# The first attention's output, row tiles 3 to 21: transposed by a crossbar transfer instead of TensorE

## The chip, the cores and the metric

The kernel runs on one core of a Trainium2 chip. The core has five engines that run at the same time, each through its own list of instructions in order: TensorE (PE, the matrix array, with its weight loads as PEld), VectorE (DVE), ScalarE (ACT), GpSimd (POOL) and SyncE (SP, which here only issues transfers). Transfers between the chip's main memory and the on-chip memory, or within the on-chip memory, run on 16 DMA engines that all queues share. Matmuls write PSUM, a small memory[...], and only VectorE and ScalarE can bring results from there to the on-chip memory in this kernel. The metric is the device time of one execution in microseconds, lower is better.

## The reference

Two attentions follow one another. The first takes q, k and v of 4 batches, 8 heads, 768 positions and 64 channels, and looks at the last 96 positions and the first 8, with a bias by distance. The second takes the first one's output x (4 x 768 x 512), routes each row to two of four experts and sums their causal attentions.

```python
scores = scale * np.matmul(q, k.transpose(0, 1, 3, 2))
keep = is_global | is_local                      # first 8 keys, or 0 <= i - j < 96
scores = np.where(keep, scores + bias, -1e9)
attn = np.matmul(softmax(scores), v)             # B, H, S, 64
x = attn.transpose(0, 2, 1, 3).reshape(B, S, 512)

logits = x @ w_gate                              # two best of four experts, softmax over the two
for e in range(4):
    q, k, v = x @ wq[e], x @ wk[e], x @ wv[e]    # 512 -> 64
    ye = causal_softmax(q @ k.T / 8) @ v @ wo[e]
    out += weight_of(e) * ye
```

## The kernel before

The 4 x 768 rows are 24 row tiles of 128, numbered u = 0 to 23, six for each batch. A row tile goes through these stages; each is a small function, and its two-letter name stands in the table that orders the work.

- *Loads* (`lk`, `lq`, `lv`, line L230): 256 KB of k, q or v each, as 128 rows of 8 heads with runs of 256 bytes. The letter at the end gives the queue that issues: `s` for SP, `a` for ACT. Each of k, q and v has six buffers.
- *Casts to fp16* (`kc`, `qc` at L250; `vc` at L258, four quarters) on POOL, VectorE or ScalarE, by the letter `g`, `v` or `a`.
- *Transposes of k and q* (`tk`, `tq`, L266) on TensorE, with one copy out of PSUM (L275).
- *Local and global scores* (`sa`, `sb`, `gs`) into PSUM tiles `sps` and `gps`, exponentials on ScalarE (L345, L318).
- *Values* (`vg`, `va`, `vb`, L356 and L371) into the PSUM tile `zps`. When the last of them is through, VectorE takes the reciprocal of the sums (L378) and multiplies (L380), which gives the row tile of x in fp16, `x16`, with three buffers.
- *Transpose of x* (`tx`, L386): four 128x128 transposes on TensorE into the PSUM tile `xps`, and one copy to `xT` (L390) on VectorE or ScalarE, also three buffers. The 512 channels are split as channel = 4c + k, so each of the four transposes reads every fourth channel of a row.
- *Projections* (`pk`, `pq`, L401; `pv` with the gate, L415): the only users of `xT`. They write the PSUM tiles `pps` and `vps`, which ScalarE or VectorE copies out.
- *Routing* (`ro`), *causal scores* (`ca`, `cb`, `cc`, L446, exponentials at L449), *mask* (`ma`, L461), *values* (`za`, `zb`, L474, again into a `zps` tile), *transpose of z* (`tz`, L491), *output* (`ou`, L502 and L505) and the store of 256 KB, issued by SP.

The order of the work is written out in the string `ORDER`, some 850 entries made by a planner. The stages are called in that order, and each engine gets its instructions in it. An engine never takes a later instruction before an earlier one, so an entry that waits holds all later entries of its engine: this holds for SP, too, where a transfer that waits holds the loads behind it.

Three pools of PSUM matter: `psS` (two buffers, scores), `psZ` (one buffer, `zps` of both attentions) and `psT` (two buffers, shared by `tp`, `xps`, `pps`, `vps`, `ztps` and `ops`).

Of the kernel before, what the change touches and what calls it, by code (L numbers as in the profile page):

```python
# [9 lines left out]
F16 = mybir.dt.float16  # L10
I32 = mybir.dt.int32
Alu = mybir.AluOpType
# [6 lines left out]
P = 128  # L19
# [3 lines left out]
def kernel(  # L23
# [7 lines left out]
    nc = tc.nc  # L31
    mm = nc.tensor.matmul
    V, S_, G = nc.vector, nc.scalar, nc.gpsimd
# [5 lines left out]
    B, H, S, Dh = q.shape  # L39
# [4 lines left out]
    NK = D // P  # L44
# [8 lines left out]
    HG = H // 2  # L53
# [7 lines left out]
    ident = const.tile([P, P], F16)  # L61
# [121 lines left out]
    pp = fast.enter_context(tc.tile_pool(name="pp", bufs=3))  # L183
# [25 lines left out]
    def held(name, u):  # L209
        t, n, owner = rings[name]  # L210
        assert owner[u % n] == u
        return t[:, u % n]
# [11 lines left out]
    fs, kqT, kgs, vgs, ags, xTs, kqs, lgs, wts, a2s, as_, done = ({} for _ in range(12))  # L224
    s16s, zs_, x16s, routing, zss, zts, tps, ppss, zs2 = ({} for _ in range(9))
# [134 lines left out]
    def local_values(u, i):  # L360


        b, ri = divmod(u, NT)
        assert done[u] > i
        for hq in (2 * i, 2 * i + 1):
            for prev in range(2 if ri else 1):
                for c in range(2):
                    for hf in range(2):
                        r = slice(hf * KB, hf * KB + KB)
                        at = c * (2 * P - KB) + prev * P  # L370
                        mm(zs_[u][:, hf, hq * VW:(hq + 1) * VW],  # L371
                           lhsT=as_[u - prev][r, hq % 2, hq // 2, at:at + P],
                           rhs=held("vbuf", u - prev)[r, c, hq, :], start=False, stop=True,
                           skip_group_check=True)
        if i == 1:
            z4 = zs_[u][:, :, 0:HG * VW].rearrange("r a (h d) -> r a h d", h=HG)
            rinv = rinv1[:, b, ri, :].rearrange("r (a h) -> r a h", a=2)
            V.reciprocal(rinv, z4[:, :, :, Dh])  # L378
            x16s[u] = pp.tile([P, 2, HG, Dh], F16, name="x16")
            V.tensor_tensor(x16s[u][:, :, :, :], z4[:, :, :, 0:Dh],  # L380
                            rinv.unsqueeze(3).to_broadcast([P, 2, HG, Dh]), op=Alu.mult)

    def turn_x(u, on):
        x_ps = psT.tile([P, NK, P], F16, name="xps", tag="t")
        for j in range(NK):
            nc.tensor.transpose(x_ps[:, j, :],  # L386
                                x16s[u][:, :, :, :].rearrange("r a h d -> r (a h d)")
                                .rearrange("r (c k) -> r k c", k=NK)[:, j, :], ident[:, :])
        xTs[u] = pp.tile([P, NK, P], F16, name="xT")
        copies[on](xTs[u][:, :, :], x_ps[:, :, :])  # L390

    def project_qk(u, i, on=None):
# [149 lines left out]
    def general_path(ctx):  # L542
# [190 lines left out]
        "tk": (turn, 0), "tq": (turn, 1), "sa": (local_scores, 0), "sb": (local_scores, 1),  # L733
        "gs": (global_scores,), "vg": (global_values,),
        "va": (local_values, 0), "vb": (local_values, 1), "tx": (turn_x,),
        "pk": (project_qk, 0), "pq": (project_qk, 1), "pv": (project_v,), "ro": (route,),
        "ca": (causal_scores, 0), "cb": (causal_scores, 1), "cc": (causal_scores, 2),
# [11 lines left out]
    for i, r in enumerate((rinv1, rinv2)):  # L749
        r = r[:, :, :, :].rearrange("p b t h -> p (b t h)")  # L750
# [22 lines left out]


ORDER = """
wi4a lq0s qc0g lk0a kc0g wm17 tk0 lv0a lk1a vc0g lq1s xt0 lk2s xb0 xg0 kc1g lq2a lk3a lq3s lq4s
qc1g tq0a wm12 vs0 az0 gi0 tk1 tq1v lk4a gs0 wm3 gs1 kc2g lv1s az1 az2 lk5s wm1 sa0 lv2s qc2g
sb0 kc3v lq5a qc3v qc4g tk2 tq2v tk3 tq3v vg0 wi0s wi1s va0 vb0 az3 az4 kc4g kc5v vc1g gs2 lv3a
lv4s vc2g sa1 sb1 wc0g tk4 wc1g tq4v vg1 sa2 sb2 lk6s wi2s va1 qc5a vb1 sa3 sb3 tx0v tk5 tq5v
vg2 va2 vb2 gs3 sa4 tx1v tx2v sb4 lq6a lq7s lk7s lk8s lv5a pk0 pk1 vc3v sa5 vc4g wc2g sb5 lq8s  # L780
kc6a lq9s lk9s lk10s pq0v pq1v vg3 va3 vb3 pk2 pq2a ca0 ca1 vg4 va4 qc6v qc7g tk6 tq6v vb4 pv0a
pv1a ca2 cb2 vg5 tx3v kc7g tk7 tq7v ma0 kc8g lv6a qc8v gi1 pk3 vc5g pq3a pv2v ro0 sa6 sb6 tx4v
ro0 qc9g tk8 tq8v kc9g va5 vb5 ca3 lq10s lq11s lk11s pv3v kc10g pv4a sa7 vc6g ro0 gs4 lv7s ma1
qc10v lv8s tk9 lq12s tq9v tk10 tq10v lk12a ro0 vs1 sb7 qc11v pk4 kc11v ro0 pq4a tx5v vg6 lq13s
vc7g va6 vb6 vc8g ro0 sa8 ro0 qc12g sb8 tk11 tq11v lk13s lk14s pv5v vg7 ca4 va7 cb3 vb7 tx6v
lq14s pk5 pq5a lq15s za0 lv9s lv10s zb0 lk15s sa9 sb9 lv11s qc13g lk16s ro1 tx7v pk6 pq6a kc12g
kc13v kc14g tk12 tq12v ro1 lq16s za1 zb1 sa10 sb10 tz0v tk13 tq13v lq17s ca5 vg8 va8 gi2 lk17s
vb8 pv6a lq18s qc14g ro1 pv7v lk18a lk19s gs5 cb4 lv12s tx8v ma2 qc15g za2 zb2 vc9g tk14 tq14v
kc15g vc10g pv8a cb5 ro1 ro1 cc4 vg9 va9 ma3 vb9 kc16g pk7 pq7a qc16v kc17g tk15 tq15v ro1
lk20s ro1 ro2 sa11 sa12 vg10 va10 vc11g vb10 gs6 tx9a wi3s tk16 tq16v qc17g qc18v sb11 sb12  # L790
lv13s lv14s za3 vc12g tx10v lq19s pk8 wc3g pq8v ma4 tz1a lq20s zb3 sa13 sa14 tz2v pk9 kc18v
pq9v kc19a pv9a vs2 vg11 va11 vb11 lk21s cc5 tk17 kc20g tq17v tk18 tq18v gi3 vg12 ca6 va12 vb12
sa15 lv15s vc13g ou0a ou1v ca7 ca8 tx11v za4 tx12v zb4 ou2a pk10 pq10v sb13 sb14 vc14g pv10v
pv11v ro2 ro2 ro2 vg13 cb8 va13 vb13 gs7 lv16s lk22s tz3a ma5 ro2 sb15 ro2 qc19g pk11 pq11a
tz4a lq21s lq22s lk23s ro2 vg14 ro3 ro3 vc15g va14 vb14 ca9 qc20g ma6 cb9 qc21g tx13v ro3 tk19
tq19v ma7 ma8 za5 zb5 ou3v ou4v sa16 sa17 kc21g vg15 va15 vb15 pv12a lv17s lv18s tx14v lv19s
sb16 sb17 za6 lv20s lq23a tk20 tq20v zb6 pv13a ca10 cb10 pk12 pq12v vc16g pk13 za7 kc22g zb7
pq13a ro3 vc17g vc18g tk21 tq21v gs8 ro3 vg16 va16 cc10 vb16 tz5a tx15v qc22g sa18 ma9 sa19
tz6v qc23g za8 zb8 ou5a ou6v ca11 ca12 ro3 vg17 va17 vb17 pk14 ro3 pq14v lv21s pv14v sb18 sb19
tz7v za9 zb9 tz8a tx16v vs3 sa20 tk22 ro4 tq22v ou7a vg18 va18 vb18 cb11 cc11 vc19g ou8v pk15  # L800
pq15v kc23g ma10 za10 zb10 pv15a lv22s tk23 tq23v sb20 sa21 tx17v ma11 ma12 za11 tx18v ro4
lv23s zb11 tz9a ro4 ca13 ro4 ma13 ca14 tz10v pk16 pq16v tz11v ca15 vg19 va19 vb19 pv16v pv17v
vc20g cb14 cb15 ro4 vg20 ro4 ro4 va20 vb20 pk17 pq17a tx19v gs9 sa22 ou9v za12 zb12 tx20a sb21
sb22 ou10v ou11a vg21 vc21g va21 vc22g vb21 ro5 sa23 sb23 vc23g pv18v pk18 za13 ro5 zb13 pq18a
ro5 ro5 pv19v ca16 ca17 ro5 ro5 vg22 va22 ro5 ma14 tz12v pk19 pq19v tx21a ca18 vb22 cb16 pk20
pq20v tx22v vg23 cc16 va23 vb23 pv20a ro6 pv21a cb17 cc17 ma15 ro6 ma16 ro6 za14 tz13v zb14
pk21 ma17 pq21v ou12a za15 zb15 ou13a ma18 tx23v ca19 ca20 ro6 tz14v ro6 tz15v za16 zb16 pv22v
pv23a cb20 ca21 ro6 ro6 za17 tz16v ro7 ro7 zb17 ou14a pk22 ma19 pq22v ro7 ro7 cb21 za18 zb18
pk23 pq23a ro7 ma20 tz17v ro7 ca22 za19 zb19 ro7 cb22 ma21 ou15v ou16v ca23 za20 zb20 tz18v
cc22 ou17v cb23 za21 zb21 ou18a tz19v ma22 cc23 za22 tz20v tz21a zb22 ou19a ou20v ma23 za23  # L810
tz22v zb23 ou21a ou22a tz23v ou23a
"""

MAXB = 512
# [38 lines left out]
```

## Time and profile before

The median of three runs is 154.23 us (153.66 to 155.45). The profiled execution spans 151.9 us.

| what | value |
|---|---|
| DMA bytes | 27.81 MB, mean 183 GB/s |
| SP's queue (q1) | 65,632 packets, 23.60 MB, 60.0% of 16 engines |
| ACT's queue (q10) | 14,704 packets, 3.68 MB, 10.8% |
| loads of k, q, v issued by SP, by ACT | 58, 14 |
| issue to landing of a load, median | 5.0 to 6.0 us |
| issue to landing of an output, median | 2.1 us |
| transposes of x (L386) | 96 matmuls, busy 9.5 us |

Busy time of an engine is the sum of its instructions' records. On TensorE the records of following matmuls overlap, so a group's busy time is not what it costs the array; the distance between starts is. "Idle before" names what the engine was waiting for ahead of a group. The line of DMA shares gives, for each of 40 equal slices, how full the 16 DMA engines were in tenths.

### The profile page before, as it was taken

Reading aid. Unit: us, or ns where it says so; the run is one execution under the profiler, and the core shown is the slowest. Engines: PE = TensorE matmul, PEld = TensorE weight load, DVE = VectorE, ACT = ScalarE, POOL = GpSimd, SP = SyncE. Lnnn points to the kernel's source line nnn. Section 1 sums busy time; section 2 is a strip of 40 time slices with the busy share of each in tenths; the row PEclk is TensorE's granted clock in tenths of the full one; section 3 lists DMA queues with packets and bytes.
Section 4 is the critical chain, followed back from the end, with each engine's and each line's share of the span. In section 5 each row is a group of like instructions: output and inputs, shape, how many; then the busy total and the mean of one; then the engine's idle time right before and its main releaser. Section 6 shows DMA issues by size and latency. Waiting matters only on the chain.

```text
span 151.9 us, 7115 instructions
## 1 busy us (share of the span) xinstructions
PE 137.3 (90%) x2987; PEld 107.5 (71%) x2987; DVE 111.3 (73%) x343; ACT 105.6 (70%) x174; POOL 94.6 (62%) x258
## 2 busy tenths in 40 slices
PE   5889969989999998899999999999999999999700
PEld 4556747768789786787787887788868987856300
DVE  6976958577887984888759788797867787797610
ACT  0345656666879887498786877869796988898410
POOL 4492896484888785749889789543786444544000
PEclk9999999999999999999999999999999999999995
DMA  4999999979899898999994994345013003116540
GB/s 106 284 288 291 353 231 279 265 177 277 195 276 233 199 239 184 204 285 223 316 242 103 261 222 135 84 147 134 4 69 145 4 4 140 73 48 230 194 167 11
DMA packets 80376, 27.81 MB, mean 183 GB/s; under 512 B 75472, under 2 KB 77008, under 8 KB 80336
## 3 DMA queue, kind: packets, MB, share of 16 engines
q1 hardware_dynamic: 65632, 23.60, 60.0%
q10 hardware_dynamic: 14704, 3.68, 10.8%
q8 instruction: 25, 0.41, 1.1%
q14 instruction: 15, 0.12, 0.3%
HBM read 20.98 MB, written 6.29 MB: 180 GB/s over the span
## 4 chain that ended last, share of the span: by engine, by line
PE 61%; DMA 11%; DVE 9%; POOL 9%; issue 3%; ACT 2%; POOLq 0%; ACTq 0%; DVEq 0%
DMA qf<-in_q_dram 11%; PE pps L401 10%; PE zps L474 7%; PE ops L502 7%; PE vps L415 6%; PE cps L446 6%; PE zps L371 4%; PE sps L335 4%; POOL vbuf L258 4%; PE tp L266 4%; PE xps L386 3%; PE sps L342 3%; PE ztps L491 2%; PE zps L356 2%; POOL s16q L250 1%
## 5 line engine op out<-in xcount | busy, mean ns | idle before, releaser
L449 ACT ACTIVATE a<-cps 128x1024 f16<-128x1024 f32 (+1 forms) x48 | 42.0, 916 | 4.0 <-PE cps L446 3.6
L258 POOL CAST vbuf<-vf 64x256 f16<-64x256 f32 x92 | 37.0, 402 | 6.6 <-DMA vf<-in_v_dram 2.6
L345 ACT ACTIVATE abuf<-sps 128x636 f16<-128x636 f32 (+1 forms) x48 | 30.7, 683 | 9.1 <-PE sps L342 8.7
L461 POOL TENSOR_SCALAR_AFFINE_SELECT a<-a 128x256 f16<-128x256 f16 x48 | 18.4, 411 | 12.8 <-ACT a L449 12.8
L275 DVE COPY kqT<-tp 128x1024 f16<-128x1024 f16 x23 | 15.5, 686 | 5.3 <-PE tp L266 5.1
L380 DVE TENSOR_TENSOR x<-zps,rinv 128x512 f16<-128x512 f32 x24 | 16.6, 691 | 0.8
L474 PE MATMUL zps<-v2buf,a 128*128 128x65 f16 x336 | 15.4, 193 | 0.2
L371 PE MATMUL zps<-vbuf,abuf 64*128 64x65 f16 x704 | 15.2, 189 | 0.0
L335 PE MATMUL sps<-biasT,ident 64*64 64x318 f16 (+1 forms) x192 | 14.8, 313 | 0.1
L401 PE MATMUL pps<-xT,wk 128*128 128x128 f16 x192 | 14.6, 219 | 0.1
L401 PE MATMUL pps<-xT,wq 128*128 128x128 f16 x192 | 14.5, 219 | 0.0
L474 PEld LDWEIGHTS <-a 128*128 128x128 f16 x336 | 12.9, 97 | 2.1 <-DVE zs L485 0.8
L371 PEld LDWEIGHTS <-abuf 64*128 64x128 f16 x704 | 13.9, 94 | 0.6
L342 PE MATMUL sps<-kqT 64*64 64x159 f16 (+2 forms) x384 | 14.2, 228 | 0.0
L415 PE MATMUL vps<-wvg,xT 128*128 128x260 f16 x96 | 13.6, 275 | 0.0
L502 PE MATMUL ops<-wo,zt 128*128 128x512 f16 x48 | 13.2, 380 | 0.4 <-DVE zt L495 0.4
L250 POOL CAST s16k<-kf 128x512 f16<-128x512 f32 x17 | 10.3, 609 | 5.2 <-DMA kf<-in_k_dram 3.3
L446 PE MATMUL cps<-kq,kq 64*128 64x128 f16 x240 | 13.2, 217 | 0.0
L446 PEld LDWEIGHTS <-kq 64*128 64x128 f16 x336 | 9.9, 94 | 4.5 <-issue 3.4
L401 PEld LDWEIGHTS <-wk 128*128 128x128 f16 x192 | 11.5, 98 | 1.8 <-issue 0.2
L342 PEld LDWEIGHTS <-kqT 64*64 64x64 f16 x384 | 11.4, 108 | 1.1 <-issue 0.2
L401 PEld LDWEIGHTS <-wq 128*128 128x128 f16 x192 | 11.6, 98 | 0.1
(112 smaller groups left out, 272.9 us busy)
## 6 DMA issues: line engine op xcount, KB each, us to landing
out_dram<-osb SPq DMA_DIRECT2D x24, 256.0 KB, 2.1
qf<-in_q_dram SPq DMA_DIRECT2D x20, 256.0 KB, 5.0
vf<-in_v_dram SPq DMA_DIRECT2D x20, 256.0 KB, 5.2
kf<-in_k_dram SPq DMA_DIRECT2D x18, 256.0 KB, 5.1
kf<-in_k_dram ACTq DMA_DIRECT2D x6, 256.0 KB, 5.3
vf<-in_v_dram ACTq DMA_DIRECT2D x4, 256.0 KB, 5.8
qf<-in_q_dram ACTq DMA_DIRECT2D x4, 256.0 KB, 6.0
w<-in_moe_wk_dram SPq DMA_DIRECT2D x1, 512.0 KB, 5.1
```

The lines of the kernel that those rows point to most:

```text
L258: copies[on](o[hf * KB:(hf + 1) * KB, c, :, 0:Dh], fs["v", u][c * KB:(c + 1) * KB, hf * HG:(hf + 1) * HG, :])
L335: mm(s_ps[o, hh, 0:2 * w].rearrange("r (c n) -> r c n", c=2), lhsT=ident2[r, :], rhs=biasT[r, p, 0:w].unsqueeze(1).to_broadcast([KB, 2, w] ...
L342: mm(s_ps[o, hh, c * w:c * w + n], lhsT=kqT[b][r, 0, p, k0:k0 + KB], rhs=kqT[b][r, 1, p, k0:k0 + n], start=False, stop=True, skip_group_ch ...
L345: S_.activation(as_[u][:, :, g, :].rearrange("r h (c n) -> r h c n", c=2)[:, :, :, 0:w], s_ps[:, :, 0:2 * w].rearrange("r h (c n) -> r h c ...
L371: mm(zs_[u][:, hf, hq * VW:(hq + 1) * VW], lhsT=as_[u - prev][r, hq % 2, hq // 2, at:at + P], rhs=held("vbuf", u - prev)[r, c, hq, :], sta ...
L401: mm(p_ps[:, i, ep, :], lhsT=w[:, ko, ep, :, :].rearrange("r a d -> r (a d)"), rhs=xT[:, ko, :], start=(i == 0 and ep == 0 and ko == 0), s ...
L415: mm(v_ps[:, :], lhsT=xT[:, ko, :], rhs=wvg16[:, ko, :], start=(ko == 0), stop=(ko == NK - 1))
L446: mm(s_ps[:, e2, i, :], lhsT=kqs[b * NT + ci][r, 0, ep, :], rhs=kqs[u][r, 1, ep, :], start=(i == 0), stop=True, skip_group_check=True)
L449: S_.activation(a2[:, :, 4 * c:4 * c + len(part), :], s_ps[:, :, 0:len(part), :], func=Exp, scale=sc2)
L461: G.affine_select(out=d, in_=d, pattern=[[0, NEP], [1, P]], channel_multiplier=-1, base=0, compare_op=Alu.is_ge, fill=0.0)
L474: mm(z_ps[:, e, :], lhsT=a2[:, e % 2, (e // 2) * n + ci, :], rhs=held("v2buf", b * NT + ci)[:, e, :], start=(e == 0 and ci == 0), stop=Tru ...
L502: mm(o_ps[:, :], lhsT=zts[u][:, ep, :], rhs=wo16[:, ep, :], start=(ep == 0), stop=(ep == NEP - 1))
```

## The change

For row tiles 3 to 21 the transpose of x is a transfer from on-chip memory to on-chip memory, issued by SP, in which the crossbar of the transfer path transposes (`dma_start_transpose`). TensorE and PSUM have no part in it, and no copy follows. Row tiles 0, 1, 2, 22 and 23 stay on TensorE.

[...]the multiply L380 now writes `x16` with the channels interleaved: k first, then c. Its neighbours in the order of reading lie 128 elements apart in the result. `x16` has five buffers instead of three and `xT` four. The table is planned anew: all stages are the same, but their order, the engines of many casts and copies, and the queues of loads differ; 24 loads of k, q and v are issued by ACT and 48 by SP, and the warm-up of the exponential (`xt0`) stands at the end of the table instead of near its start.

```diff
-            x16s[u] = pp.tile([P, 2, HG, Dh], F16, name="x16")
-            V.tensor_tensor(x16s[u][:, :, :, :], z4[:, :, :, 0:Dh],
-                            rinv.unsqueeze(3).to_broadcast([P, 2, HG, Dh]), op=Alu.mult)
+            x16s[u] = pp.tile([P, NK, P], F16, name="x16", bufs=5)
+            V.tensor_tensor(x16s[u][:, :, :].rearrange("r k (a h d) -> r a h d k", a=2, h=HG),
+                            z4[:, :, :, 0:Dh].rearrange("r a h (d k) -> r a h d k", k=NK),
+                            rinv.unsqueeze(3).unsqueeze(4)
+                            .to_broadcast([P, 2, HG, Dh // NK, NK]), op=Alu.mult)
 
     def turn_x(u, on):
+
+        xTs[u] = pp.tile([P, NK, P], F16, name="xT", bufs=4)
+        if on == "s":
+            nc.sync.dma_start_transpose(xTs[u][:, :, :],
+                                        x16s[u][:, :, :].rearrange("r k c -> r (k c)"))
+            return
         x_ps = psT.tile([P, NK, P], F16, name="xps", tag="t")
         for j in range(NK):
-            nc.tensor.transpose(x_ps[:, j, :],
-                                x16s[u][:, :, :, :].rearrange("r a h d -> r (a h d)")
-                                .rearrange("r (c k) -> r k c", k=NK)[:, j, :], ident[:, :])
-        xTs[u] = pp.tile([P, NK, P], F16, name="xT")
+            nc.tensor.transpose(x_ps[:, j, :], x16s[u][:, j, :], ident[:, :])
         copies[on](xTs[u][:, :, :], x_ps[:, :, :])
```

Of the table, the entries around the transposes of row tiles 3 to 6 (the letter `s` marks the transfer):

```diff
-pv1a ca2 cb2 vg5 tx3v kc7g tk7 tq7v ma0 kc8g lv6a qc8v gi1 pk3 vc5g pq3a pv2v ro0 sa6 sb6 tx4v
-ro0 qc9g tk8 tq8v kc9g va5 vb5 ca3 lq10s lq11s lk11s pv3v kc10g pv4a sa7 vc6g ro0 gs4 lv7s ma1
-qc10v lv8s tk9 lq12s tq9v tk10 tq10v lk12a ro0 vs1 sb7 qc11v pk4 kc11v ro0 pq4a tx5v vg6 lq13s
+lq8a lk8s pq1v qc7g vg3 va3 tx2v vb3 tx3s lv5s ca0 lv6a tk6 tq6v wc2g ca1 tk7 tq7v vc4v lk9a
+vg4 lq9s pk2 pq2a sa6 gi1 sb6 qc8g pv0v pv1v va4 vb4 tx4s lq10a ca2 cb2 kc8g tk8 tq8v pk3 ma0
+ma1 lk10s pq3a vg5 sa7 lv7a sb7 vc5v vc6g pv2v kc9g lk11s ro0 ro0 pv3v gs4 va5 vb5 tx5s vs1
+qc9g tk9 lv8s ro0 ro0 pk4 tq9v pq4v vg6 va6 lq11s lq12a qc10g vb6 sa8 tx6s sb8 kc10g pv4v tk10
```

More of the change, by code (lines that the diff above doesn't have):

```diff
@@ L775 @@
 ORDER = """
[L776 to L781, printed above, removed]
@@ L782 @@
-pv1a ca2 cb2 vg5 tx3v kc7g tk7 tq7v ma0 kc8g lv6a qc8v gi1 pk3 vc5g pq3a pv2v ro0 sa6 sb6 tx4v
-ro0 qc9g tk8 tq8v kc9g va5 vb5 ca3 lq10s lq11s lk11s pv3v kc10g pv4a sa7 vc6g ro0 gs4 lv7s ma1
-qc10v lv8s tk9 lq12s tq9v tk10 tq10v lk12a ro0 vs1 sb7 qc11v pk4 kc11v ro0 pq4a tx5v vg6 lq13s
-vc7g va6 vb6 vc8g ro0 sa8 ro0 qc12g sb8 tk11 tq11v lk13s lk14s pv5v vg7 ca4 va7 cb3 vb7 tx6v
-lq14s pk5 pq5a lq15s za0 lv9s lv10s zb0 lk15s sa9 sb9 lv11s qc13g lk16s ro1 tx7v pk6 pq6a kc12g
-kc13v kc14g tk12 tq12v ro1 lq16s za1 zb1 sa10 sb10 tz0v tk13 tq13v lq17s ca5 vg8 va8 gi2 lk17s
@@ L788 @@
[L788 to L811, printed above, removed]
+lk0s lk1a kc0g wm17 tk0 az0 xb0 az1 lq0s lq1a az2 lv0a xg0 lk2s lk3a kc1a qc0g qc1g lq2s lq3a
@@ new lines @@
+wm7 tq0a qc2v tk1 wm1 tq1a wm7 sa0 vc0g az3 sb0 kc2g wm2 tk2 lk4s gi0 vs0 tq2v kc3g qc3g tk3
+kc4v lq4s qc4g lv1s vc1g lk5s kc5g gs0 gs1 lq5s lv2a vc2g tq3v sa1 sb1 wi0a wi1s lv3s vg0 va0
+vb0 tk4 sa2 wm1 vg1 lk6s lk7s az4 tq4v tx0v qc5v gs2 sb2 sa3 va1 wc0g vb1 tk5 tq5v lq6a sb3
+tx1v vc3g vg2 va2 lq7a gs3 sa4 qc6g wi2s wc1v vb2 sb4 wi4s pk0 pk1 pq0v sa5 sb5 kc6v kc7g lv4a
+lq8a lk8s pq1v qc7g vg3 va3 tx2v vb3 tx3s lv5s ca0 lv6a tk6 tq6v wc2g ca1 tk7 tq7v vc4v lk9a
+vg4 lq9s pk2 pq2a sa6 gi1 sb6 qc8g pv0v pv1v va4 vb4 tx4s lq10a ca2 cb2 kc8g tk8 tq8v pk3 ma0
@@ new lines @@
+ma1 lk10s pq3a vg5 sa7 lv7a sb7 vc5v vc6g pv2v kc9g lk11s ro0 ro0 pv3v gs4 va5 vb5 tx5s vs1
+qc9g tk9 lv8s ro0 ro0 pk4 tq9v pq4v vg6 va6 lq11s lq12a qc10g vb6 sa8 tx6s sb8 kc10g pv4v tk10
+tq10v vc7g ro0 lk12s vc8g kc11v vg7 qc11g ca3 ca4 ro0 lv9s ro0 lv10s lk13a va7 vb7 qc12g pk5
+pq5v pv5v sa9 sb9 ma2 vg8 va8 vb8 lq13s cb3 kc12g tx7s lk14s vc9g tk11 tq11v kc13g pk6 pq6v za0
+zb0 tx8s lq14a sa10 gs5 tk12 lv11s tq12v ro1 pv6a sa11 sb10 tz0v vg9 va9 qc13v vb9 ro1 cb4
+vc10g tx9s gi2 tk13 tq13v pv7v ca5 qc14v vg10 va10 vb10 lq15s lv12s cc4 pv8a kc14g tk14 ro1
@@ new lines @@
+vc11g lk15a tq14v sa12 tx10s sb11 za1 zb1 lk16a pk7 pq7v pv9a ma3 cb5 lq16s vg11 lq17s vc12g
+va11 vb11 ro1 gs6 ro1 pk8 pq8v tz1a qc15v lk17s kc15v kc16g sa13 qc16g vs2 za2 pk9 pq9a lq18s
+tx11s tk15 ro1 lv13a qc17g lv14s ro1 tq15v lk18s zb2 sb12 sb13 ro2 kc17g ro2 pk10 pq10v tk16
+tq16v wi3s ca6 vg12 va12 vb12 tx12s ro2 ca7 tk17 tq17v pv10a ro2 ma4 sa14 sb14 za3 zb3 vc13g
+tz2v lk19s lk20a pk11 ro2 kc18g sa15 lv15s ro2 lq19s lq20s sb15 pq11v wc3g pv11v vc14g cc5
+lv16a lv17s vg13 lq21s qc18g ma5 va13 vb13 ca8 ou0v ou1v cb8 ma6 kc19g lk21a za4 zb4 pk12 ro2
@@ new lines @@
+pq12a qc19v ro3 tk18 tq18v kc20v sa16 sb16 qc20g vg14 lk22s va14 tx13s vb14 sa17 tz3v tk19 ro3
+tq19v ca9 cb9 tx14s tz4v vc15g za5 zb5 ou2a tk20 tq20v gs7 sa18 za6 ro3 zb6 ou3a vc16g ou4v
+lv18s ca10 ro3 vg15 va15 vb15 kc21g kc22g cb10 pv12v pv13v cc10 qc21g lv19s vg16 va16 vb16 ca11
+tx15s tz5v pk13 pq13a ma7 lq22a za7 zb7 sb17 lv20s sb18 tz6v lq23s tk21 lv21s tq21v ma8 za8 zb8
+pv14a gi3 sa19 sa20 pk14 ro3 pq14v tz7v ma9 ro3 vg17 vc17g vc18g va17 tx16s lv22s cb11 vb17
+ou5a ou6v ro3 ro4 tx17s sb19 sb20 za9 pv15v qc22v zb9 vc19g tz8a gs8 ro4 vs3 tk22 pk15 tq22v
@@ new lines @@
+vc20g pq15a ma10 ca12 vc21g vg18 lk23s lv23s ro4 va18 vb18 cc11 pv16v pv17v ro4 tx18s ro4 za10
+qc23v zb10 ma11 ou7a sa21 ro4 ro4 sb21 pk16 pq16v tz9v vg19 ca13 ro5 kc23g va19 vb19 ca14 tk23
+ma12 ma13 tq23v pk17 pq17v cb14 vg20 va20 vb20 sa22 sb22 tx19s tx20s tz10v pv18v za11 ro5 zb11
+ro5 ou8a ou9v gs9 za12 zb12 ou10a pv19v ca15 cb15 vc22g ma14 za13 vc23g zb13 pk18 pq18v tz11v
+ca16 ro5 ro5 vg21 va21 vb21 ca17 pv20v pk19 pq19v cb16 ro5 cc16 ro5 ro6 vg22 va22 vb22 ro6 ro6
+tz12v pk20 pq20a sa23 sb23 tx21s tz13v ro6 ro6 za14 zb14 pk21 pq21a tx22v cb17 vg23 va23 ro6
@@ L812 @@
+vb23 ou11a ou12v cc17 ma15 ma16 ma17 ro6 za15 zb15 tz14a ou13v ca18 ca19 ma18 tx23v za16 zb16
+pv21a pv22v ca20 cb20 pv23v ro7 za17 tz15v zb17 ro7 tz16v ro7 ro7 ro7 ca21 cb21 pk22 ma19 ma20
+ma21 pq22v pk23 ro7 pq23a ro7 za18 zb18 ca22 ou14v ou15a za19 zb19 ca23 tz17v cb22 tz18v za20
+zb20 ou16v cc22 ou17a za21 ma22 zb21 cb23 cc23 ma23 tz19v ou18v tz20v za22 zb22 ou19a ou20v
+tz21v za23 tz22a zb23 ou21a ou22a tz23v ou23a xt0
 """
```

## Prediction

> **What bounds the kernel now.** I read the shares of the engines first, then the stretches of 20 us, then the chain that ended last, then the timeline around two of the transposes that the change takes away, then the transfer queues. The engine shares and slices say that TensorE is the fullest engine and that the transfers are full for a good half of the run:
>
> ```profile
> PE 137.3 (90%) x2987; PEld 107.5 (71%) x2987; DVE 111.3 (73%) x343; ACT 105.6 (70%) x174; POOL 94.6 (62%) x258
> ...
> PE   5889969989999998899999999999999999999700
> ...
> DMA  4999999979899898999994994345013003116540
> ```
>
> The stretches, with columns PE, weight load, DVE, ACT, POOL, granted clock, DMA share and GB/s, show the same in time:
>
> ```profile
> 0.00:20.00 20.00, 17.05 (x244) 11.88 (x245) 15.94 (x56) 8.22 (x14) 12.47 (x34) 1.00 1.10 266
> 20.00:40.00 20.00, 17.80 (x408) 14.10 (x409) 13.42 (x35) 13.47 (x24) 13.36 (x34) 1.00 1.04 240
> 40.00:60.00 20.00, 19.77 (x506) 16.78 (x504) 15.29 (x44) 16.55 (x29) 16.42 (x44) 1.00 1.00 225
> 60.00:80.00 20.00, 19.09 (x453) 15.44 (x453) 15.20 (x43) 15.40 (x29) 15.36 (x40) 1.00 1.00 250
> 80.00:100.00 20.00, 20.00 (x484) 15.88 (x482) 16.54 (x47) 15.94 (x28) 14.94 (x39) 1.00 0.61 155
> ```
>
> Up to 40 us TensorE has gaps (17.05 and 17.80 of 20) and the DMA engines have none (share 1.10 and 1.04); from 40 to 80 us both are full; from 80 us on TensorE alone is. The chain agrees: it goes through transfers of q rows three times (14.4 to 21, 24.8 to 30.3, 57.9 to 62.7 us) and from 64 to 143 us hardly leaves TensorE.
>
> ```profile
> PE 61%; DMA 11%; DVE 9%; POOL 9%; issue 3%; ACT 2%; POOLq 0%; ACTq 0%; DVEq 0%
> ```
>
> Counting each matmul by the usual distance to the next start in a dense run (56 ns for 128 columns, 111 for 260, 216 for 512, 29 and 15 ns for the two kinds of 65 columns, and so on) gives 117 us of array time in all: 63 to 76% of the first 40 us, 80 to 92% of the time from 40 to 140.
>
> So TensorE work removed after 40 us should come off the end, provided nothing else starts to hold TensorE; work removed before 40 us should not.
>
> **What a transpose costs TensorE.** Records of matmuls overlap (220 ns each in the groups), so I take the distance between starts:
>
> ```profile
> 71.08 0.41 PE L386 MATMUL xps<-ident,x 128*128 128x128 f16 x4
> 71.33 0.47 PE L474 MATMUL zps<-v2buf,a 128*128 128x65 f16 x10
> 71.63 0.39 PE L386 MATMUL xps<-ident,x 128*128 128x128 f16 x4
> 71.86 0.47 PE L474 MATMUL zps<-v2buf,a 128*128 128x65 f16 x10
> ```
>
> Four transposes hold the array for 0.25 and 0.23 us; I use 0.24 us for a row tile. The groups name the two VectorE operations around them:
>
> ```profile
> L380 DVE TENSOR_TENSOR x<-zps,rinv 128x512 f16<-128x512 f32 x24 | 16.6, 691 | 0.8
> ...
> L390 DVE COPY xT<-xps 128x512 f16<-128x512 f16 x21 | 8.7, 420 | 2.5 <-PE xps L386 2.3
> ```
>
> **What the Trainium skill says.** "DMA: Bandwidth & Descriptors", section "Latency and other measured facts", gives crossbar transposes 261 GB/s with non-contiguous middle dims and 350 to 400 when contiguous. "VectorE: DVE Perf Modes", section "The three transpose paths", gives 1309 ns for one 128x128 tile by the crossbar. No trace of the kernel before has a crossbar transpose. The first page's section "Issuing engines are not separate DMA queues" says that all issuers share the same 16 engines; the trace agrees, since the share falls from 1.22 to 0.15 only as the loads run out, whoever issued them. "Advanced Engine Details and Errata", section "SBUF Cachelines", says that accesses that touch another 16-byte line each time pay a penalty. The trace before has no VectorE write of that kind; the nearest thing, weight loads that read x with 8-byte steps, takes 113 ns against 97 to 98 for packed ones.
>
> **The change, part by part.**
>
> *Removed from TensorE:* 19 row tiles x 0.24 us = 4.6 us. The transposes before 40 us make some 5 to 6 row tiles, of which rows 0 to 2 stay as they are; so about 3 of the 19 fall where TensorE has gaps anyway. 16 x 0.24 = 3.8 us come off the part that is full.
>
> *Removed from the copies:* 16 copies of xT on VectorE (16 x 0.42 = 6.8 us) and 3 on ScalarE (3 x 0.58 = 1.7 us). The replanned table spends it again: VectorE gets 6 more copies of v2buf (2.5), 2 of kq (1.4), 3 of zt (0.9), 4 quarter casts of v (1.4), 4 of wq (about 1.6, by POOL's 0.39 each), one of q (0.5), and one kqT fewer (-0.7): +7.6, so VectorE stays where it was. ScalarE loses 6 of v2buf, 2 of kq, 3 of zt and more, some 6 us in all, and issues 25 loads instead of 15, 10 x 0.4 = 4 us. I cost all this at nothing: these engines are 70 to 73% busy and TensorE covers them. The freed PSUM pair of xps (two buffers are shared by six uses per row, now five) can only help; I leave it out.
>
> *Table call for the activation tables moved to the end:* the first ScalarE cast loads the table instead, and it stands in front of a wait for the first k load. Nothing. The 1-element activation at the end runs beside the checks of the sums on VectorE. Nothing.
>
> *The multiply (L380)* writes the same 512 elements, but each one 256 bytes from the last. At one element a cycle it stays 0.69 us. If every write costs two, the slope 1.04 ns per element (from 691 and 424 ns for 512 and 256 elements) doubles: 1.22 us. I take 0.69 and give the other end to a rival.
>
> *Added: 19 transposes of 128 KB on SP's queue.* Low end: 128 KB at 261 GB/s = 0.5 us of the engines. High end: four times 1309 ns = 5.2 us. I take about 1 us on the queue and 2 to 3 us from issue to landing with nothing ahead (the 256 KB outputs land in 2.1). 19 x 1 = 19 us on SP's queue, which now holds 60% of 152 = 91 us. The ten loads that move to ScalarE's queue take about 10 x 1.4 = 14 us off it (91 us over 65,632 packets = 1.4 us for a load of 1,024). About even, and hidden.
>
> *Added waits.* A transpose on SP's in-order queue waits for the multiply of its row and for an xT buffer (four of them, for row u-4). Behind it stand loads of k, q, v for later rows; their casts on POOL and VectorE, then turn on TensorE, wait in turn. Before, loads were issued as soon as buffers came free; now they go in step with L380. By adding the array times above along both tables, the load of a k row from row 12 to 18 stands 3 to 7 us of TensorE work before its cast now, 4 to 10 before. The medians of issue to landing are 5 us while the queue is full, so there is little to spare, but a queue that is fed less far ahead is also less full. The other wait is projection for the transposed row: from the last matmul into zps to the first projection lie 4.3 us of TensorE work at the tightest rows (4 and 5) and 5 to 10 elsewhere. The chain needs 0.2 + 0.69 + handoffs 0.3 + issue 1 + landing 2 to 3 = 4.2 to 5.2 us; at the 70 to 80% density of that stretch 4.3 of work last 5.5 to 6. It fits, with nothing left if two loads are ahead in the queue.
>
> **Forecast:** 154.2 - 3.8 = 150.4 us.
>
> **Rivals.**
>
> 1. *The waits take it back.* Ten rows, 3 to 12, fall while the queue is full; if each holds TensorE for 0.35 us, 3.5 us return: 153.9 us, no change. For it: landings of 5 us in this stretch. Against it: fewer loads ahead in the queue.
>
> 2. *The strided multiply is twice as long.* zps has one buffer, so the next values stage waits for L380. In the new table 0.7 to 2.6 us of TensorE work (median 1.4) stand between; the hold is about 1.2 us now and would be 1.7. An average stall of 0.35 us x 24 = 8 us: 154.2 - 3.8 + 8 = 158.4 us, slower. For it: the page on cachelines. Against it: at one element a cycle of 2 bytes the port is far from its peak.
>
> 3. *The crossbar is slow.* At 2.6 us for a row (half the high end) SP's queue carries 91 - 14 + 50 = 127 us, most of it beside the loads, and the path to the projection becomes about 7 us against 5 to 6: 1 to 1.5 us for each of the 10 early rows, 12 us, or 154.2 - 3.8 + 12 = 162.4. At 5.2 us the queue alone holds 176 us. For it: the 1309 ns. Against it: that price must hold a fixed part.
>
> 4. *The freed PSUM buffer and the new table give more.* By the array times above, some 27 us up to the last matmul are not work; a tenth of it (2.7) and the full 4.6: 147 us.
>
> **How the numbers follow.** Forecast 0.50, rival 4 0.06: faster 0.56. Rival 1 0.13: within 1%. Rival 2 0.14, rival 3 0.17: slower 0.31. The range goes from 147 (rival 4) to 160, beyond which lies most of rival 3 and nothing else.
>
> **What would show it.** Right: xps falls to 20 matmuls, the 3.8 us is gone between 40 us and the end, L380 stays near 0.69 us, transposes land in under 4 us, and the waits of projection for xT are few. Rival 1 shows as pps or vps waiting for the transfer of xT; rival 2 as L380 near 1.2 us and zps waiting for it; rival 3 as long landings and SP busy in them, with casts waiting for loads behind. The forecast is wrong above all if a step of the transpose that no trace here shows is mis-sized.

## Result and profile after

The changed kernel takes 180.66 us (median of 4 runs, 179.71 to 183.22) against 153.94 us before (now of 4 runs, too): a ratio of 1.174 (95% interval 1.162 to 1.186). It is 27 us slower where a gain of 4 was forecast, and 20 us beyond the upper end of the range.

The profiled execution spans 181.5 us. It is the slowest of the four by 2 us (its granted clock is 0.94 in the mean, 0.97 in the others), so the gaps counted below are a little large; ratios here and below leave such executions out, medians keep them. First the shares of the engines and the slices, the same lines as before:

```profile
PE 138.9 (77%) x2913; PEld 105.8 (58%) x2913; DVE 148.7 (82%) x346; ACT 101.1 (56%) x159; POOL 93.0 (51%) x251
...
PE   6875979677768777897785976976949866999820
...
DVE  7888598989999999888958698789897988788730
```

TensorE has 74 recorded matmuls fewer and falls from 90% to 77%. VectorE has about as many instructions as before and 37 us more work: it is now the fullest engine. The row of nines that TensorE had is gone. Two stretches from 40 us on (columns PE, weight load, DVE, ACT, POOL, granted clock, DMA share, GB/s):

```profile
40.00:60.00 20.00, 15.14 (x390) 12.53 (x389) 19.09 (x34) 10.30 (x16) 10.94 (x28) 1.00 0.89 179
60.00:80.00 20.00, 16.11 (x391) 13.24 (x392) 18.30 (x39) 12.47 (x22) 12.66 (x32) 1.00 0.90 189
```

TensorE got through 390 matmuls from 40 to 60 us, 506 before. The chain that ended last says where the time went; its shares by engine are

```profile
PE 39%; DVE 39%; DMA 11%; ACTq 3%; issue 2%; POOL 1%; ACT 1%; SPq 0%; POOLq 0%; DVEq 0%
```

VectorE's share of the chain was 9% and is 39%; its largest single item is the multiply L380 with 28%. The groups show why:

```profile
L380 DVE TENSOR_TENSOR x<-zps,rinv 128x512 f16<-128x512 f32 x24 | 58.5, 2438 | 0.8
...
L479 PE MATMUL zps<-v2buf,a 128*128 128x65 f16 x336 | 15.2, 195 | 11.0 <-DVE x L380 9.0
...
L356 PE MATMUL zps<-vg,ag 64*128 64x260 f16 x48 | 7.0, 287 | 9.8 <-DVE x L380 8.5
```

The multiply takes 2438 ns instead of 691: 24 x 1.747 = 42 us more on VectorE. The next values, of either attention, need the one `zps` buffer and wait for it. The view of TensorE's waits (total, times, longest) gives 8 + 8 such waits by name:

```profile
PE zps L479 <- DVE x L380: 9.0, 8, 1.6
PE zps L356 <- DVE x L380: 8.5, 8, 1.4
```

By the starts in the trace it is more rows still: at 20 of the 24, the next matmul into `zps` starts within 0.2 us of the end of the multiply, at 7 before. The other waits of this kind are put down to a small VectorE operation that stands behind the multiply.

A piece of the chain from 64 us, in order of time (start, length, what), shows the alternation. TensorE does the work that the table put between two users of `zps`, and the rest of its list stands behind the waiting one:

```profile
63.77 0.51 PE zps L371 x32
64.30 0.22 DVE rinv L378
64.54 2.44 DVE x L380
...
73.05 0.50 PE zps L371 x32
73.58 0.22 DVE rinv L378
73.82 2.44 DVE x L380
76.31 0.34 PE zps L479 x6
```

By starts of matmuls plus their usual distances (the prediction's way of counting), the gaps over 0.15 us in TensorE's work sum to 9.9 us in the profile before and 42.6 us after; 24.3 us of the latter lie in front of a `zps` matmul (0.5 before). The array time itself went from 116.6 to 112.6 us, so the 4 us that the change was to save were saved; they are invisible behind 33 us of new gaps.

The transfers did what was expected of them (issue on SP's queue: shortest, median, longest in ns; then the time to landing):

```profile
L389 SPq DMA_TRANSPOSE xT<-x x19: 1190/1201/2820, 35.7 to 144.8; - x19
...
DMA to landing us min/median/max: 2.4/4.0/6.7
```

### The profile page after: what moved, and what is told of

It is laid out like the page before. It is cut to its first block, busy times and chain, and to the rows that moved or that the text cites. A ratio compares the mean times of both kernels' runs of the same rounds, so it can differ in the third digit from the quotient of the medians.

```text
span 181.5 us, 6995 instructions
## 1 busy us (share of the span) xinstructions
PE 138.9 (77%) x2913; PEld 105.8 (58%) x2913; DVE 148.7 (82%) x346; ACT 101.1 (56%) x159; POOL 93.0 (51%) x251
## 2 busy tenths in 40 slices
DMA packets 90711, 30.29 MB, mean 167 GB/s; under 512 B 85808, under 2 KB 87344, under 8 KB 90672
## 4 chain that ended last, share of the span: by engine, by line
PE 39%; DVE 39%; DMA 11%; ACTq 3%; issue 2%; POOL 1%; ACT 1%; SPq 0%; POOLq 0%; DVEq 0%
DVE x L380 28%; DMA qf<-in_q_dram 8%; PE pps L406 6%; PE zps L479 6%; PE zps L371 4%; PE ops L507 4%; DMA vf<-in_v_dram 3%; PE cps L451 3%; PE vps L420 3%; ACTq L230 3%; PE sps L335 3%; DVE rinv L378 2%; DVE kqT L275 2%; PE sps L342 2%; PE ztps L496 2%
## 5 line engine op out<-in xcount | busy, mean ns | idle before, releaser
L380 DVE TENSOR_TENSOR x<-zps,rinv 128x512 f16<-128x512 f32 x24 | 58.5, 2438 | 0.8
L258 POOL CAST vbuf<-vf 64x256 f16<-64x256 f32 x88 | 35.5, 403 | 12.8 <-DMA vf<-in_v_dram 9.2
L275 DVE COPY kqT<-tp 128x1024 f16<-128x1024 f16 x22 | 16.8, 769 | 2.5 <-PE tp L266 2.4
L371 PE MATMUL zps<-vbuf,abuf 64*128 64x65 f16 x704 | 16.0, 194 | 0.0
L406 PE MATMUL pps<-xT,wk 128*128 128x128 f16 x192 | 15.4, 227 | 0.2 <-DVE kqT L275 0.2
L371 PEld LDWEIGHTS <-abuf 64*128 64x128 f16 x704 | 14.6, 97 | 1.2 <-issue 0.8
L356 PE MATMUL zps<-vg,ag 64*128 64x260 f16 x48 | 7.0, 287 | 9.8 <-DVE x L380 8.5
L250 POOL CAST s16q<-qf 128x512 f16<-128x512 f32 x16 | 9.8, 617 | 9.1 <-DMA qf<-in_q_dram 8.4
L250 POOL CAST s16k<-kf 128x512 f16<-128x512 f32 x18 | 11.1, 621 | 5.0 <-DMA kf<-in_k_dram 4.8
L411 DVE CAST kq<-pps 128x512 f16<-128x512 f32 x15 | 10.6, 709 | 3.1 <-PE pps L406 3.0
```

Of the source, the lines that this page charges most:

```text
L250: copies[on](s16s[nm, u][:, :, :], fs[nm, u][:, :, :])
L258: copies[on](o[hf * KB:(hf + 1) * KB, c, :, 0:Dh], fs["v", u][c * KB:(c + 1) * KB, hf * HG:(hf + 1) * HG, :])
L275: copies[on](kqT[b][:, :, :, ri * P:(ri + 1) * P], tps[u][:, :, :, :])
L371: mm(zs_[u][:, hf, hq * VW:(hq + 1) * VW], lhsT=as_[u - prev][r, hq % 2, hq // 2, at:at + P], rhs=held("vbuf", u - prev)[r, c, hq, :], sta ...
L380: V.tensor_tensor(x16s[u][:, :, :].rearrange("r k (a h d) -> r a h d k", a=2, h=HG), z4[:, :, :, 0:Dh].rearrange("r a h (d k) -> r a h d k ...
L406: mm(p_ps[:, i, ep, :], lhsT=w[:, ko, ep, :, :].rearrange("r a d -> r (a d)"), rhs=xT[:, ko, :], start=(i == 0 and ep == 0 and ko == 0), s ...
```

## The experiments

My theory after the result: the write order of the multiply is the whole loss; each element is written 256 bytes from the last, and that costs 3.5 times, not 1 or 2. Rivals: the short inner runs of four cost it, not the distance; the transfers; the new table.

**1. The forms of the operation by themselves.** This kernel leaves both attentions out and only runs the multiply, copies and transfers in several forms, four times each.

> Leaves out both attentions: it only times the disputed operation in several forms, four times each, and stores a tile to the output. Theory A (each write that steps to another 16-byte line costs extra): the multiply with packed writes takes 0.69 us; writes 4 and 8 bytes apart stay near 0.7; 16, 32 and 64 bytes apart rise to 2.4 us like the interleaved one; groups of four packed writes with a gap between stay near 0.7. Theory B (short innermost rows of 4 cost a start each, whatever they write): groups of four packed writes take about 2.4 us and writes far apart in long rows stay at 0.7. Reading PSUM out of order with packed writes, in two halves: 0.85 us if only writes suffer, 2 us or more if reads suffer the same. The crossbar transfer alone: 1.2 us on the queue, 2 to 3 us to land.

The groups, each shape apart. `xo<-z` with 512 elements holds four packed and four interleaved ones (4 x 691 + 4 x 2432 ns = 12.5 us), `xf` is an fp32 result, `zs` a source in on-chip memory, the 256-element form reads PSUM out of order and writes packed, L92 and L94 are ScalarE copies, interleaved and packed, L86 and L89 VectorE copies of fp16. The two lines of `big` are the groups with steps of 8 and 16 bytes, each from a window of its own:

```profile
L59 DVE TENSOR_TENSOR xo<-z,rinv 128x512 f16<-128x512 f32 x8 | 12.5, 1561 | 0.3
L92 ACT CAST xo<-z 128x512 f16<-128x512 f32 x4 | 9.7, 2432 | 75.5 <-DVE xo L89 75.4
L59 DVE TENSOR_TENSOR xo<-zs,rinv 128x512 f16<-128x512 f32 x4 | 9.7, 2423 | 0.0
L86 DVE COPY xo<-zh 128x512 f16<-128x512 f16 x4 | 5.2, 1306 | 0.1
L59 DVE TENSOR_TENSOR xf<-z,rinv 128x512 f32<-128x512 f32 x4 | 5.0, 1243 | 0.0
L59 DVE TENSOR_TENSOR xo<-z,rinv 128x256 f16<-128x256 f32 x8 | 2.9, 439 | 0.0
L94 ACT CAST xo<-z 128x512 f16<-128x512 f32 x4 | 2.3, 585 | 0.1
...
L89 DVE COPY xo<-zh 128x512 f16<-128x512 f16 x4 | 1.2, 294 | 0.1
```

```profile
L59 DVE TENSOR_TENSOR big<-z,rinv 128x512 f16<-128x512 f32 x4 | 5.2, 1290 | 0.1
...
L59 DVE TENSOR_TENSOR big<-z,rinv 128x512 f16<-128x512 f32 x4 | 9.7, 2419 | 0.1
```

| fp16 result of 512 elements, written | ns |
|---|---|
| packed; or in groups of four packed with a gap behind each | 691; 691 |
| every 2nd element (4-byte step) | 726 |
| every 4th (8) | 1290 |
| every 8th, 16th, 32nd (16, 32, 64) | 2419, 2293, 2377 |
| interleaved as in the change (256-byte step inside groups of four) | 2432 |

Groups of four cost nothing when each group is packed, so short runs are not it. The step between consecutive writes is: nearly free at 4 bytes, 1.9 times at 8, 3.3 to 3.5 times from 16 on. (At 8 bytes theory A had expected no cost.) Reading out of order costs nothing: two of the 256-element forms, with a 16-byte step in PSUM, start 0.33 us apart, while a packed 512-element form starts every 0.73 us. The source does not matter either: read from on-chip memory, the interleaved form takes 2423 ns.

The Trainium skill's page "Advanced Engine Details and Errata", section "SBUF Cachelines", names 16-byte lines and a penalty for another line at each access; the rise up to 16 bytes and its end there agree. Its remark that at least two hits on a line are needed must not be read as two being enough: at 8 bytes each line gets two, and the operation still takes 1290 ns. A price for each new line would fit the series: from 8 to 16 bytes the lines that 512 elements touch double from 256 to 512, and 1129 ns more make 4.4 ns a line, an estimate from these two figures and the page's line; packed or at 4 bytes (64 or 128 lines) that is under 0.6 us, less than the operation takes anyway. But the fp32 result and the fp16 copy touch a new line with each element, too, and take half as long (1243 and 1306 ns), so the count of lines alone does not give the time. What in the engine or the memory sets it stays open.

A transfer by itself takes 1.19 us on the queue and 2.4 us to land, and 0.6 to 0.7 us of the 16 engines.

**2. One part alone: the interleaved multiply in the kernel before,** with its own table and all transposes on TensorE (the four weight loads of a row then read packed channels).

```diff
-V.tensor_tensor(x16s[u][:, :, :, :], z4[...], ...)                  # packed
+V.tensor_tensor(x16s[u].rearrange("r k (a h d) -> r a h d k", ...), z4[...], ...)
```

> The kernel before with its table and its TensorE transposes, but with the interleaved multiply. Theory A (the multiply at 2.4 us holds the one zps buffer): each of 24 row tiles holds TensorE some 1 to 1.5 us more, 174 to 190 us. Rival (the transfers and the queue they stand in made the kernel slow): the multiply is hidden, 154 to 159 us.

182.95 us, ratio 1.188 (1.181 to 1.196): the multiply alone costs 29 us, without any transfer and without the new table. Shares and the group of this kernel:

```profile
PE 141.2 (77%) x2987; PEld 109.7 (60%) x2987; DVE 147.5 (80%) x343; ACT 106.0 (58%) x174; POOL 94.6 (52%) x258
```

```profile
L380 DVE TENSOR_TENSOR x<-zps,rinv 128x512 f16<-128x512 f32 x24 | 58.6, 2441 | 0.8
```

They are close to those of the changed kernel. Its gaps in front of `zps` sum to 26.5 us, and 5.3 us more lie in front of `xps`, which here waits for the multiply, too.

**3. The change with the multiply mended.** The channels stay interleaved, but the instruction reads PSUM out of order and writes packed, in two halves of 256:

```diff
-V.tensor_tensor(x16s[u].rearrange("r k (a h d) -> r a h d k", ...), z4 (d k) ..., ...)
+for a in range(2):
+    V.tensor_tensor(x16s[u][:, :, a*64:(a+1)*64].rearrange("r k (h d) -> r k h d", ...),
+                    z4[:, a, :, 0:Dh].rearrange("r h (d k) -> r k h d", k=NK), ...)
```

> The changed kernel with one edit: the multiply writes packed and reads PSUM out of order instead, in two halves (0.83 us for both by the forms measured). Theory A2 (what is left of the loss is in the table and in what waits behind the transfers): 158 to 163 us, as the natural-order kernel (160.6). Rival (the weights in shorter runs cost the natural-order kernel its 7 us): 149 to 154 us.

157.84 us, ratio 1.030 (1.017 to 1.043): 22.8 of the 26.7 us are gone. The multiply, now two instructions, takes 0.84 us for a row:

```profile
L381 DVE TENSOR_TENSOR x<-zps,rinv 128x256 f16<-128x256 f32 x48 | 18.1, 419 | 1.0 <-DVE rinv L378 0.2
```

The kernel is still slower than before, so the write order is not all of it. Two waits of TensorE in this kernel:

```profile
PE vps L422 <- DMA xT<-x: 3.5, 4, 1.9
PE ops L509 <- POOL wo L174: 2.8, 1, 2.8
```

No wait for the multiply is left in this view; the projections wait for transfers (landing at a median of 4.6 us here, 7.2 at most), and one output waits for `wo`, whose load stands behind a transfer on SP's queue. I also undid the interleaving altogether: channels split as 128k + c, the weights loaded to match, multiply as before.

> The changed kernel with channels in natural order: weights loaded so that channel = 128k + c, so that the multiply writes packed and the transfer still transposes contiguous blocks. Theory A: the multiply is back at 0.69 us and the time falls to 148 to 153 us, at or below the kernel before. Rival (transfers): 165 us or more, with waits for xT and for loads behind the transfers.

160.55 us, ratio 1.043 (1.035 to 1.051), where 148 to 153 us had been expected if the multiply were the whole loss. This kernel has one fault of its own: the weights then arrive in short pieces (92,336 packets under 512 B against 85,808). The same edit put into the kernel before measures that:

> The kernel before with weights loaded in natural channel order and nothing else changed. Theory A2: 153 to 155.5 us. Rival (the weights in shorter runs are the cost): 157 us or more.

155.72 us, ratio 1.016 (1.008 to 1.024). So some 2 us of the 160.55 come from the weights, and the two mended kernels agree. Both say that the multiply is most of the loss and not the whole.

**4. What is left: the new table, or the transfers?** I ran the new table with the transposes on TensorE. Left at the places of the transfers, right behind the values (and with the weights of the natural order, which cost some 2 us), they wait for the multiply:

> The same as the natural-order kernel with its new table, but row tiles 3 to 21 transposed by TensorE with a copy on VectorE. Theory A: 2 to 5 us slower than the natural-order kernel with transfers, about 152 to 157 us: what the transfer itself brings. Rival (transfers cost more than they bring): faster than the natural-order kernel with transfers.

166.25 us, ratio 1.083 (1.076 to 1.089), where 152 to 157 us had been expected. That measures the place more than the table: the weight loads of the transposes wait 8.6 us for the multiply. With each transpose moved to some 0.9 us of array time ahead of its first use, and the multiply of before:

> The new table with the multiply and the TensorE transposes of before, those of row tiles 3 to 21 placed about 0.9 us of TensorE work ahead of their first use, so that they don't wait for the multiply. If the new table itself costs: 158 us or more. If what waits for and behind the transfers is what is left of the loss: 152 to 156 us.

160.58 us, ratio 1.043 (1.031 to 1.055). So the table with the transposes put back costs some 6.6 us, and the transfers, against it, bring 2.7 us by the medians (160.58 to 157.84), 2.0 by the ratios, with an uncertainty as large. The 6.6 us are not a price of the table alone: it was planned without these transposes and without their copies, which bring VectorE to 117.6 us of work against 111.3 before. Four more kernels ask which part of the table it is: the distance of the transposes, the queues of the loads, the engines of casts and copies (72 of 673 entries differ), or all of these letters, which leaves the order alone.

> The new table with the transposes of rows 3 to 21 on TensorE, now about 1.8 us of array time ahead of their first use instead of 0.9. If the 7 us that the new table cost in its first form came from transposes placed too close to their use, this gives 154 to 157 us. If they belong to the table itself, it stays at 159 to 162.

> The new table's order, transposes on TensorE 0.9 us ahead of use, and each load on the queue that it had in the old table (14 loads of k, q, v from ScalarE's queue instead of 24). If the loads that ScalarE now issues cost the 7 us, this gives 154 to 157 us; if the order or the engines of the casts and copies do, 159 to 163.

> The new table's order and queues, transposes on TensorE 0.9 us ahead of use, and each cast and copy on the engine that it had in the old table (72 entries differ). If the assignment of casts and copies costs the 7 us, this gives 154 to 157 us; if the order does, 159 us or more, since these letters were not chosen for this order.

> The new table's order alone, with both the queues and the engines of the old table. If the order is the cause, this stays at 159 us or above; if queues and engines together are, it comes to 154 to 156.

| transposes on TensorE, order of the new table | ratio to before | interval |
|---|---|---|
| 0.9 us ahead of use | 1.043 | 1.031 to 1.055 |
| 1.8 us ahead of use | 1.049 | 1.035 to 1.063 |
| queues of the old table | 1.047 | 1.040 to 1.055 |
| engines of the old table | 1.086 | 1.077 to 1.094 |
| both of the old table | 1.110 | 1.098 to 1.123 |

None comes near 1. Distance and queues make no difference that these runs can tell, and the old engines make it worse, though VectorE then has only 110.6 us of work: its extra copies alone don't explain the loss. But these engines had been chosen for another order, so the row does not clear the new ones. What is left over is the order itself, in which TensorE's transposes had no place planned; that is argued, not shown. In the first of these kernels the gaps are 15.7 us instead of 9.9, and spread (3.2 us in front of `xps`, 2.7 `ops`, 2.6 `tp`, 2.4 `pps`). No single wait carries them.

**5. Can the loads be moved out of the way?** In the mended change the load of `wo` stands behind the transfer of row 11; I moved it ahead of that of row 8.

> The changed kernel with the multiply that reads out of order, and one entry of its table moved: the load of wo stands ahead of the transfer of row tile 8 instead of behind that of row tile 12. If loads that stand behind transfers on SP's queue are part of the loss: the 3 to 4 us wait of the first output for wo goes, 153.5 to 156 us against 157.8. If the wait only moves elsewhere: 157 to 159 us.

158.97 us (154.8 to 161.58), too scattered for a ratio. The wait for `wo` shrank (gaps in front of `ops` from 4.1 to 1.1 us), those of projections for `xT` grew (5.0 to 6.9): inconclusive. The wait only moved, as far as one profile tells.

**6. Transfers in the old table,** with the multiply that writes packed, placed right behind the values. First rows 14 to 21, then with the loads of v17 to v20 moved ahead of the transfers, then with rows 10 to 13 too:

> The table of before; only row tiles 14 to 21, whose transposes lie where few loads are left, go by transfer, issued right behind their values, with the multiply that reads out of order. If the saving of TensorE is real where nothing waits behind a transfer: 8 x 0.24 = 1.9 us off, 151 to 153 us. If a transfer costs wherever it stands: 155 us or more.

> The table of before with row tiles 14 to 21 by transfer, as before, but the loads of v for row tiles 17 to 20 moved ahead of the transfers that they stood behind. If the one 4 us wait of POOL for v was what took the saving back: 151 to 153 us. Rival (TensorE's saving is not on the path there at all): 153.5 to 155 us.

> As the kernel with the loads moved ahead, and row tiles 10 to 13 by transfer too, which fall where the transfer queues are full. If a transfer there holds nobody: 12 x 0.24 = 2.9 us off the kernel before, 150 to 152.5 us. If loads queued behind it come late: 154 us or more.

| rows by transfer | ratio to before | interval | medians, and before beside them, us |
|---|---|---|---|
| 14 to 21 | 1.0042 | 1.0002 to 1.0083 | 153.98, 153.58 |
| 14 to 21, loads ahead | 1.0041 | 1.0005 to 1.0076 | 154.00, 154.93 |
| 10 to 21, loads ahead | 1.0090 | 1.0056 to 1.0124 | 155.15, 154.93 |

A gain of 1 to 2% was expected and did not come, though each row takes 0.24 us off TensorE. All three lie within 1% of the kernel before. In the second the ratio and the medians point to different sides, so not even the sign of its effect is shown. In the first, POOL waited 4.1 us for a v row whose load was issued at 84.56 us behind a transfer at 83.27; moving the loads ahead removed that wait, and the ratio stayed.

So I looked at single packets. In the kernel before no packet of 256 bytes took over 68 ns, and 18 ns is usual. In the mended change 174 on SP's queue took over 200 ns (up to 2.2 us; together 10.9 us of all 16 engines), and 41 on ScalarE's; in the kernel of rows 14 to 21 with loads ahead, 36 and 5. The packets of a transfer have 256 bytes, too, so some of those on SP's queue may be its own; ScalarE's queue carries no transfers, and its slow packets belong to loads. All of them start within 5 us of the issue of a transfer. In the mended change none come after the last load has landed; with rows 14 to 21 or 10 to 21 by transfer, 7 or 8 do, of up to 1.7 us; in the kernel of experiment 1, with transfers alone, no packet of 256 bytes took over 53 ns. A kernel that leaves the attentions out was to price this, with loads alone, transfers alone and both:

> Leaves out both attentions: it loads 24 tiles of 256 KB in five stages apart from one another (from SP alone; the same with a crossbar transfer after every third load; eight transfers alone; the loads from SP and ACT in turn; the same with transfers). Theory C (a transfer beside loads stalls DMA engines in single packets of 1 to 2 us): the second stage is 8 x 1.2 to 1.9 = 10 to 15 us longer than the first, with packets over 200 ns, and the fifth longer than the fourth by the same. Rival (a transfer takes only its bytes, 0.6 us of the engines): 5 us longer, and no long packet.

The stages ran into one another from 53 us on, where ScalarE's queue started early, so only the stretch before it is clean. Loads from SP alone take 1.14 us each (27 in 30.9 us); then a transfer follows every third load:

```profile
32.88 1.82 SPq L49 DMA_TRANSPOSE xT<-xo  x1
34.80 2.12 SPq L46 DMA_DIRECT2D kf<-in_k_dram  x3
36.97 1.54 SPq L49 DMA_TRANSPOSE xT<-xo  x1
...
49.08 1.78 SPq L49 DMA_TRANSPOSE xT<-xo  x1
```

From 32.88 to 49.08 lie four rounds, 4.05 us each, against 3 x 1.14 = 3.4: 0.6 us for a transfer, which is about what it needs of the 16 engines by itself. So with one queue of loads the slow packets cost no throughput that this run can tell; with two queues it does not tell. As far as it goes it speaks for the smaller of the two expected prices. What a transfer among loads costs in the kernel would then be its share of the engines, in a stretch where their share is 1.0, and the later landing of what queues behind it, not a stall of the whole; no run has measured this in the kernel. That leaves a test: transfer only the rows that come when few loads are left, 18 to 21.

> The table of before; only row tiles 18 to 21 by transfer, whose transfers fall behind nearly all loads. Theory C: no packets over 200 ns to speak of, and 4 x 0.24 = 1.0 us off, 0.3 to 0.9% faster than before. Rival (the saving is not on TensorE's path at all): the same as before or slower, like row tiles 14 to 21 (0.4% slower).

153.83 us against 154.65, ratio 0.994 (0.990 to 0.999): faster by 0.6%, as expected. The medians say the same (0.995). But so do those of rows 14 to 21 with loads ahead (0.994), so these runs do not show that the loads make the difference between the two. Its transfers land early, at 2.7 us at the median (the line gives shortest, median and longest), and hardly a packet is slow (five of 256 bytes took over 200 ns, the longest 326):

```profile
DMA to landing us min/median/max: 2.4/2.7/3.3
```

## Why the prediction was wrong

**The bound was right.** TensorE held the kernel before, and what took it away from its work showed at the end almost in full: some 31 us more gaps in front of `zps` and `xps` in the kernel of experiment 2, 29 us more time.

**The step that failed: "At one element a cycle it stays 0.69 us. If every write costs two, ... 1.22 us. I take 0.69 and give the other end to a rival."** It is 2.44 us, and at this length it holds the one `zps` buffer and with it TensorE (shown: put into the kernel before it costs 29 us, taken out of the change it gives 22.8 back). Both ends were below the truth: "two per write" was a guess at a worst case, with no row behind it, and weight loads at 8-byte steps (113 ns against 97), which I named as the nearest thing, are reads by another engine. The page on cachelines pointed the right way but gave no number, so the upper end was not known, and the range could not rest on it. Rival 2 had the mechanism: `zps` has one buffer and its next user waits. It reckoned a hold of 1.7 us against 0.7 to 2.6 us of work and 8 us of stalls; the hold is 2.9 (0.2 + 2.44 + handoffs), and the stalls are 24 us. Its own working with 2.9 gives 2.9 - 1.4 = 1.5 us of stall at each of 24 rows, 36 us, and 186 us in all: somewhat over the result, but on the right side by far. The mechanism stood in the prediction; the term was mis-sized, and the chance of 0.14 with it.

**Right in size:** `xps` fell to 20 matmuls, and the array time by 4.0 us. A transfer takes 1.2 us on the queue (about 1 predicted) and lands in 2.4 us with nothing ahead (2 to 3), 4.0 at the median. Rival 3, with 2.6 us on the queue and more, falls. VectorE's other work evened out: 111.5 us busy in the mended change, 111.3 before. (16 x 0.42 is 6.7 us, not 6.8; nothing rests on it.)

**The table, costed at nothing, does cost something:** 6.6 us with the transposes put back into it, as experiment 4 measured it. I compared the busy shares of the engines and did not ask whether the new order has as few gaps as the old. That it is the order is what four variants leave over; no single wait accounts for it, and no test has changed the order piece by piece. This stays open.

**The added waits** were named rightly ("nothing left if two loads are ahead"), and in the mended change they are there: 3.5 us of `vps` waiting for `xT` and 2.8 us for `wo`. They may be what takes back part of the 3.8 us, of which 2 to 2.7 remain by experiment 4; that they are is not shown.

The sum by medians: 153.9 before, + 6.6 for the table, - 2.7 for the transfers, + 22.8 for the writes = 180.6 us. It closes because each term is the difference of two neighbouring kernels; in the table before, the same writes cost 29 us, so the terms depend on the order in which they are taken.

## What to carry to other kernels

A layout that a transfer reads is best made by the reads of the instruction before it: PSUM read out of order cost nothing here, fp16 writes with a step of 16 bytes or more cost 3.3 to 3.5 times. Where one buffer stands between a producer and that instruction, multiply its extra time by the number of tiles before looking at anything that the change saves, and where the trace has no row for a form, leave the upper end open. Transposes by transfer saved little here even with the write order mended: 0.6% for the four rows behind nearly all loads, no clear gain for eight, and none for twelve.

## What was not expected of the hardware

- The step between consecutive fp16 writes sets the time of this VectorE multiply: 691 ns packed, 726 at 4 bytes, 1290 at 8, 2293 to 2432 from 16 on, for 128x512. A ScalarE copy pays the same when interleaved: 2432 against 585. With an fp32 result the interleaved form takes 1243, half of the fp16 one; an fp16 copy without PSUM goes from 294 to 1306.
- Near a transfer with transpose, single packets of 256 bytes are slow, some of them of loads: over 200 ns and up to 2.6 us in the changed kernel, where 18 ns is usual and 68 the most without such transfers. What makes them slow was not found, and their cost with two loading queues was not measured.
